# SSM tables: last sums of the X table on TensorE and ScalarE, wide Y products, attention masks and turns in halves

## The chip, the cores, the metric

One core of one Trainium2 chip. The time is that of one execution on the device in microseconds (us), smaller is better; every run here counted as fast but one, of the kernel before in the third and fourth group of experiments (530.97 us, over 1.5% above the fastest of its group); it is left out of the ratios. Times of runs and of the profile differ a little: the profiled run of the kernel before took 526.4 us (span 524.6), the median of its timed runs is 528.6.

## The reference

Two kinds of layer alternate, twice each, on x of 2048 positions and 512 channels (cut to what matters):

```python
def _A_ref(u, A_re, A_im, B_re, B_im, C_re, C_im, log_dt, Dskip):   # SSM convolution
    dt = jnp.exp(log_dt)[:, None]
    ...
    P = jnp.exp(logdA[:, :, None] * l[None, None, :])
    K = jnp.einsum("dn,dnl,dn->dl", Cc, P, dB).real                 # filter of 2048 taps, N = 128 modes
    ...
    y = irfft(rfft(u, 2 * L) * rfft(K, 2 * L))[:L]                   # long convolution
    return y + u * Dskip

def _B_ref(x, wqkv, wo):                                            # 32 heads, window 8, dilation 2
    ...

x = x + _A_ref(_layernorm(x), ...)
x = x + _B_ref(_layernorm(x), ...)
x = x + _A_ref(_layernorm(x), ...)
x = x + _B_ref(_layernorm(x), ...)
```

## The kernel before

The filter K is built in the first layer only. For each of eight groups of 64 channels (tables 0 to 7) VectorE builds a table X (32 powers), a base of a table Y (16 powers) and three times two products of that base; TensorE contracts X with Y in 256 small matmuls (the contraction), and ScalarE copies what comes of it to KTq (its evacuation). Beside it runs the convolution: transform matmuls (`s1`), Z copies on ScalarE, DMA transposes (`turn`), 16 matmuls of the second step (`s2`), copies to Kt (filter) or to xc and W (input), filter products pa and pb on VectorE (`products`), inverse matmuls, VT copies, final matmuls.

```python
def turn(nc, zt, Z, g0, n):
    for r in range(2):
        nc.sync.dma_start_transpose(zt[:, r, 0:n * 128]..., Z[:, r, g0:g0 + n, :]...)

# Conv: all of it draws on one PSUM pool, psA, of three buffers
def s1(self, rhs_j, n, drow=None):
    Z = self.z.tile([128, 2, 16, 128], BF, name="Z", tag="Z")          # two buffers before
    for jq in range(NJ // 4):
        ps = self.pst([128, 2, 16, 32])                                # psA
        ...                                                            # 8 matmuls
        self.evac("z", Z[:, :, 0:n // 8, jq * 32:(jq + 1) * 32], ps[:, :, 0:n // 8, :])   # ScalarE
    return Z

# Tables
def double(self, T, m, lev, hc):                                       # HALF = 8
    for e0 in range(0, m, HALF):
        ...
        nc.vector.tensor_tensor(v(ta), src, self.mult(self.MA, lev, hc, mm), ALU.mult)
        nc.vector.tensor_tensor(v(tb), src, self.mult(self.MB, lev, hc, mm), ALU.mult)
        nc.vector.tensor_tensor(T[...], ta[...], tb[:, ::-1, ...], ALU.add)

def half(hc, between=None):
    Xt, Y, Y2 = T.build(hc)                                            # Y: one buffer, X: two
    ...
    T.x_part(Xt, hc); T.y_base(Y, hc); T.y_products(Y, Y2, hc)
    r = between() if between is not None else None                     # the next s1, turn, s2
    with tc.high_priority():
        T.contract(Xt, Y, Y2, hc)                                      # frees Y
    return r

for dc in range(4):
    Kt = half(dc * 2, (lambda: k_fft(dc - 1)) if dc > 0 else None)
    if dc > 0:
        VT = cv.finish(dc - 1, xcs.pop(dc - 1), Kt, Xr, dc < 3)        # products, inverse, final
    if dc < 3:
        half(dc * 2 + 1, mid)                                          # mid: u_fft(dc + 1)
```

The order of instructions on an engine is chosen when the kernel is built, by a scheduler with priorities; at run time each engine works through its own list in that order.

## Time and profile before

| | before |
|---|---|
| median of three runs (lowest, highest) | 528.58 us (528.37, 529.04) |
| span of the profiled run, mean granted TensorE clock | 524.6 us, 0.934 |
| busy share: TensorE, VectorE, ScalarE | 73%, 82%, 67% |
| first Kt copy of table 7, here called the end of the table stage | 228.7 us |

```profile
PE 31%; DVE 28%; ACT 7%; DMA 5%; issue 5%; POOL 2%; SPq 2%; ACTq 0%; DVEq 0%; POOLq 0%
```

ScalarE is busy for only 2 to 6 tenths from slice 6 to slice 17, in the stage, and in many of these slices the clock falls to 6 to 8 tenths. The chain goes through TensorE and VectorE in nearly equal parts.

### The profile page before, as it was taken

To read this page: it belongs to the slowest core of one execution; us is meant where nothing else is said; L and a number is where in the kernel's file an instruction comes from. 1 tells how busy PE (TensorE), PEld (TensorE's weight loads), DVE (VectorE), ACT (ScalarE), POOL (GpSimd) and SP (SyncE) were. 2 spreads that over 40 slices of the span, in tenths; PEclk is the share of its full clock that TensorE was granted. 3 is DMA by queue.
4 is the path that set the end of the run, shared out by engine and by line. 5 is a ranking of instruction groups with operands and counts; after the bars stand their busy time and mean duration, and the time that the engine had idled before them with its cause. 6 is when DMAs were issued, how large, how long until landed. Compare 5 with 4: busy or idle time off the path is not lost.

```text
span 524.6 us, 15316 instructions
## 1 busy us (share of the span) xinstructions
PE 383.4 (73%) x6456; PEld 255.8 (49%) x6518; DVE 432.8 (82%) x974; ACT 350.1 (67%) x422; POOL 83.3 (16%) x135
## 2 busy tenths in 40 slices
PE   0200466568469555879898999987799989999996
PEld 0100324346246423656565565655566646666674
DVE  4999999989998998969696566887689999666663
ACT  3999825636265543635676777867788777888872
POOL 0000000000000003051146411134000214911110
PEclk9999998779688967979999899998899999999999
DMA  8301044363446257531437743424397004633532
GB/s 266 144 1 40 1 101 79 65 109 126 105 75 155 44 121 136 191 40 49 164 99 147 153 107 81 72 18 172 73 197 161 1 11 94 126 107 84 101 93 92
DMA packets 104826, 52.52 MB, mean 100 GB/s; under 512 B 86004, under 2 KB 100469, under 8 KB 103477
## 3 DMA queue, kind: packets, MB, share of 16 engines
q1 hardware_dynamic: 103044, 50.88, 42.2%
q8 instruction: 51, 0.84, 0.7%
q10 hardware_dynamic: 1584, 0.39, 0.4%
q0 software_dynamic: 128, 0.26, 0.1%
q14 instruction: 19, 0.15, 0.1%
HBM read 17.96 MB, written 8.13 MB: 50 GB/s over the span
## 4 chain that ended last, share of the span: by engine, by line
PE 31%; DVE 28%; ACT 7%; DMA 5%; issue 5%; POOL 2%; SPq 2%; ACTq 0%; DVEq 0%; POOLq 0%
PE psG L1090 5%; ACT PT L1127 5%; PE psG L1107 4%; PE S L1124 4%; PE O L1143 3%; DVE Ytab L660 3%; DVE Y2tab L662 3%; PE psG L1182 3%; DMA zt<-Z 3%; DVE ln_st_b L216 2%; DVE ta L623 2%; PE S L1182 2%; DVE tb L624 2%; DMA xt<-xq 2%; POOL XU L1262 1%
## 5 line engine op out<-in xcount | busy, mean ns | idle before, releaser
L1127 ACT ACTIVATE PT<-S 128x1824 bf16<-128x1824 f32 x72 | 121.7, 1690 | 35.1 <-PE S L1124 34.6
L1090 PE MATMUL psG<-XU,wqk 128*128 128x512 bf16 x196 | 56.3, 384 | 2.6 <-issue 1.5
L1095 DVE CAST st<-psG 128x512 bf16<-128x512 f32 x56 | 38.5, 688 | 21.0 <-PE psG L1090 20.5
L1143 PEld LDWEIGHTS <-PT 128*128 128x128 bf16 x1152 | 38.9, 96 | 13.0 <-DVE on L1151 1.5
L1107 PE MATMUL psG<-wv,XU 128*128 128x256 bf16 x288 | 40.7, 274 | 0.2 <-DVE st L1095 0.2
L1143 PE MATMUL O<-V,PT 128*128 128x17 bf16 x1120 | 38.9, 171 | 2.0 <-DVE on L1151 1.3
L311 PE MATMUL psA<-X,sb_F 128*128 128x128 bf16 x128 | 13.8, 242 | 36.4 <-ACT X L724 35.2
L311 PEld LDWEIGHTS <-sb_F 128*128 128x128 bf16 x256 | 16.9, 105 | 44.1 <-issue 41.8
L1124 PEld LDWEIGHTS <-KS 32*128 32x128 bf16 x1152 | 20.5, 93 | 28.4 <-issue 23.3
L298 ACT CAST Z<-psA 128x1024 bf16<-128x1024 f32 (+1 forms) x32 | 28.8, 987 | 7.5 <-PE psA L311 7.5
L679 PE MATMUL psk<-Ytab,Xtab 128*32 128x64 bf16 x1024 | 24.0, 209 | 12.0 <-issue 6.8
L1124 PE MATMUL S<-QS,KS 32*128 32x114 bf16 x1152 | 28.1, 211 | 6.1 <-DMA KS<-st 2.8
L336 PE MATMUL psA<-zt,sb_C 128*128 128x512 bf16 x30 | 14.9, 524 | 23.3 <-DMA zt<-Z 23.3
L1151 DVE TENSOR_TENSOR on<-O,rd 128x256 bf16<-128x256 f32 x70 | 29.7, 425 | 2.4
L682 PE MATMUL psk<-Y2tab,Xtab 128*32 128x48 bf16 x1024 | 23.3, 205 | 11.2 <-issue 9.1
L660 DVE TENSOR_TENSOR Ytab<-Ytab,MA 128x2048 bf16<-128x2048 bf16 (+1 forms) x33 | 30.6, 929 | 0.2
L662 DVE TENSOR_TENSOR Y2tab<-Ytab,MB 128x2048 bf16<-128x2048 bf16 (+1 forms) x33 | 30.6, 928 | 0.0
L688 ACT CAST KTq<-psk 128x1024 bf16<-128x1024 f32 (+1 forms) x9 | 8.3, 918 | 33.1 <-issue 32.5
L637 POOL MEMSET Xtab<- 128x64 bf16 x8 | 1.6, 200 | 180.2 <-PE psk L682 161.4
L1107 PEld LDWEIGHTS <-XU 128*128 128x128 bf16 x288 | 25.3, 98 | 6.9 <-issue 0.2
L682 PEld LDWEIGHTS <-Xtab 128*32 128x32 bf16 x1024 | 20.9, 102 | 15.7 <-issue 14.8
L679 PEld LDWEIGHTS <-Xtab 128*32 128x32 bf16 x1024 | 21.4, 107 | 13.0 <-issue 12.2
(252 smaller groups left out, 1060.8 us busy)
## 6 DMA issues: line engine op xcount, KB each, us to landing
kt_scratch<-Kt SPq DMA_DIRECT2D x4, 1024.0 KB, 3.9
Kt<-kt_scratch SPq DMA_DIRECT2D x4, 1024.0 KB, 5.0
QS<-st SPq DMA_DIRECT2D x58, 64.0 KB, 1.9
KS<-st SPq DMA_DIRECT2D x58, 64.0 KB, 1.9
X<-in_A_u_dram SPq DMA_DIRECT2D x4, 512.0 KB, 5.5
out_dram<-X SPq DMA_DIRECT2D x16, 128.0 KB, 1.7
k_scratch<-KTq SPq DMA_DIRECT2D x7, 256.0 KB, 2.5
KT<-k_scratch SPq DMA_DIRECT2D x7, 256.0 KB, 2.8
```

What stands on the lines that cost most here:

```text
L311: nc.tensor.matmul(o, F1[:, j, r, :], rhs_j(j), start=True, stop=not dk)
L660: nc.vector.tensor_tensor(v(Y[:, :, :, q * EYB:(q + 1) * EYB, :]), src, vm(self.mult(self.MA, lev, hc, EYB)), ALU.mult)
L662: nc.vector.tensor_tensor(v(Y2[:, :, :, (q - 1) * EYB:q * EYB, :]), src, vm(self.mult(self.MB, lev, hc, EYB)), ALU.mult)
L679: nc.tensor.matmul(psk[32 * g:32 * g + 32, ds, :], xs, Y[:, m // 2, h, :, t], start=(m == 0), stop=False, skip_group_check=True)
L682: nc.tensor.matmul(psk[32 * g:32 * g + 32, ds, EYB:], xs, Y2[:, 1 - m // 2, h, :, t], start=False, stop=(m == 3), skip_group_check=True)
L1090: nc.tensor.matmul(ps[:], wqk[:, ct, f0:f0 + 128], xnT[:, ct, par, UF + h * 512:UF + h * 512 + 512], start=(ct == 0), stop=(ct == 3))
L1095: eng(t[:], ps[:])
L1107: nc.tensor.matmul(ps[:].rearrange("p h d -> p (h d)"), xnT[:, ct, par, NQ * b + 1:NQ * b + 1 + NK], wv[:, ct, fp * 256:fp * 256 + 256], s ...
L1124: nc.tensor.matmul(S[:, i, sl * NQ:(sl + 1) * NQ], KS[r, e, f2, b * NQ + 1:b * NQ + 1 + NK], QS[r, e, f2, UF + b * NQ:UF + b * NQ + NQ], s ...
L1127: nc.scalar.activation(pt[:, 0:16 * NQ].rearrange("k (i x) -> k i x", i=4), S[:, :, 0:4 * NQ], ACT.Exp, scale=DH ** -0.5)
L1143: nc.tensor.matmul(O[:, x * 8 + i * 2 + e, :], pt[:, c0:c0 + 128], V[:, par * NB + b, (fp * 2 + f2) * 8 + i * 2 + e, :], start=True, stop= ...
L1151: nc.vector.tensor_tensor(on.rearrange("q (h d) -> q h d", d=DH), O[:, :, 0:DH], rd[:].unsqueeze(2).to_broadcast([128, 16, DH]), ALU.mult)
```

## The change

The intent is to take work off VectorE, which has the highest busy share. Its parts: (a) three operations of the coefficients move into a wait at the start; (b) another layout of Y and of the multipliers lets two products of 6144 elements replace six of 2048; (c) the last X doubling becomes two multiplies of 2048 into X and a buffer `xb` of its own, whose sum TensorE forms with an identity and ScalarE copies back (tables 1 to 7); (d) the second X column is copied by ScalarE; (e) in the attention layer the mask loads come two at a time and the transposes of late key rows are issued in halves at two steps. To make room, Z gets one buffer instead of two. The core of the diff:

```diff
+    def double_last(self, X, lev, hc, cv):
+        nc, m = self.nc, EX // 2
+        tb = cv.z.tile([128, 2, HD, m, 2], BF, name="xb", tag="xb")
+        ...
+        nc.vector.tensor_tensor(X[top half], src, self.mult(self.MA, lev, hc, m), ALU.mult)
+        nc.vector.tensor_tensor(tb, src, self.mult(self.MB, lev, hc, m), ALU.mult)
+        if hc == 0:
+            nc.vector.tensor_tensor(top, top, tb[:, ::-1]..., ALU.add)
+            return
+        for c in range(2):
+            ps = cv.pst([128, 2, 512])                       # psA, as all transforms
+            for q in range(2):
+                for k, t in ((0, X[top half]), (1, tb[:, 1 - c, hs])):
+                    nc.tensor.matmul(ps[:, q, :], cv.C["ident"][:], t..., start=(k == 0), stop=(k == 1))
+            nc.scalar.copy(X[:, c, :, m:, :]..., ps[:]...)
...
-        for lev in range(1, 5):
+        for lev in range(1, 4):
             self.double(X, 1 << lev, 6 + lev, hc)
+        self.double_last(X, 10, hc, cv)
...
-        cv = Conv(nc, tc, es, C, X, psA, ())
+        cv = Conv(nc, tc, es, C, X, psA, (), zbufs=1)
...
-                if 1 <= t <= 4 and Wt["todo"] or t == 8 and Wt["todo"]:
-                    Wt["todo"].pop()()
-                for g, steps in ((2, (1, 2, 4, 6)), (3, (4, 5, 6, 8))):
+                for _ in range({1: 2, 2: 2, 8: 1}.get(t, 0)):
+                    if Wt["todo"]:
+                        Wt["todo"].pop()()
+                for g, steps in ((2, (1, 2, (3, 5), 6)), (3, (4, 5, (6, 7), 8))):
```

More of the change, by code (lines that the diff above doesn't have):

```diff
@@ L518, in ladder @@
     nc.vector.tensor_tensor(ws[:], tb[:], rnd[:], ALU.subtract)
+    t1, t2 = tmp("t1"), tmp("t2")
+    nc.vector.tensor_tensor(t1[:], raw["C_re"][:], raw["B_re"][:], ALU.mult)
+    nc.vector.tensor_tensor(t2[:], raw["C_im"][:], raw["B_im"][:], ALU.mult)
+    nc.vector.tensor_tensor(t1[:], t1[:], t2[:], ALU.subtract)
     sh = tmp("sh")
@@ L540, in coefs @@
     def coefs():
-        t1 = tmp("t1")
-        t2 = tmp("t2")
-        nc.vector.tensor_tensor(t1[:], raw["C_re"][:], raw["B_re"][:], ALU.mult)
-        nc.vector.tensor_tensor(t2[:], raw["C_im"][:], raw["B_im"][:], ALU.mult)
-        nc.vector.tensor_tensor(t1[:], t1[:], t2[:], ALU.subtract)
         nc.vector.tensor_tensor(quad[:, :, 0, :], t1[:], dt_bc, ALU.mult)
@@ L565, in multipliers @@
             return
-        nc.scalar.copy(MA[:, i], src[:, 0].unsqueeze(2).to_broadcast([128, 8, 2, 64]))
+        nc.scalar.copy(MA[:, :, i], src[:, 0].unsqueeze(2).to_broadcast([128, 8, 2, 64]))
         conj = 7 <= i <= 10
-        nc.scalar.activation(MB[:, i, :, 0, :], src[:, 1], ACT.Copy, scale=-1.0 if conj else 1.0)
-        nc.scalar.activation(MB[:, i, :, 1, :], src[:, 1], ACT.Copy, scale=1.0 if conj else -1.0)
+        nc.scalar.activation(MB[:, :, i, 0, :], src[:, 1], ACT.Copy, scale=-1.0 if conj else 1.0)
+        nc.scalar.activation(MB[:, :, i, 1, :], src[:, 1], ACT.Copy, scale=1.0 if conj else -1.0)
     cur = LAM
@@ L608, in mult, with pair @@
     def mult(self, M, lev, hc, n):
-        return (M[:, lev, hc].rearrange("n c (h t) -> n (c h) t", t=2).unsqueeze(2)
+        return (M[:, hc, lev].rearrange("n c (h t) -> n (c h) t", t=2).unsqueeze(2)
                 .to_broadcast([128, 2 * HD, n, 2]))
+    def pair(self):
+        return self.wk.tile([128, 2, 2, HD, HALF * 2], BF, name="tab", tag="tab")
     def double(self, T, m, lev, hc):
@@ L616, in double @@
             mm = min(m, HALF)
-            ta = self.wk.tile([128, 2, HD, HALF * 2], BF, name="ta", tag="ta")
-            tb = self.wk.tile([128, 2, HD, HALF * 2], BF, name="tb", tag="tb")
+            both = self.pair()
+            ta, tb = both[:, 0], both[:, 1]
             def v(t):
-                return t[:].rearrange("n c h (e t) -> n (c h) e t", t=2)[:, :, 0:mm, :]
+                return t.rearrange("n c h (e t) -> n (c h) e t", t=2)[:, :, 0:mm, :]
             src = T[:, :, :, e0:e0 + mm, :].rearrange("n c h e t -> n (c h) e t")
@@ L626, in double, with x_part @@
                                     ta[:, :, :, 0:mm * 2], tb[:, ::-1, :, 0:mm * 2], ALU.add)
+    def double_last(self, X, lev, hc, cv):
+        nc, m = self.nc, EX // 2
+        tb = cv.z.tile([128, 2, HD, m, 2], BF, name="xb", tag="xb")
+        src = X[:, :, :, 0:m, :].rearrange("n c h e t -> n (c h) e t")
+        nc.vector.tensor_tensor(X[:, :, :, m:, :].rearrange("n c h e t -> n (c h) e t"), src,
+                                self.mult(self.MA, lev, hc, m), ALU.mult)
+        nc.vector.tensor_tensor(tb[:].rearrange("n c h e t -> n (c h) e t"), src, self.mult(self.MB, lev, hc, m), ALU.mult)
+        if hc == 0:
+            top = X[:, :, :, m:, :].rearrange("n c h e t -> n c h (e t)")
+            nc.vector.tensor_tensor(top, top, tb[:, ::-1].rearrange("n c h e t -> n c h (e t)"), ALU.add)
+            return
+        for c in range(2):
+            ps = cv.pst([128, 2, 512])
+            for q in range(2):
+                hs = slice(16 * q, 16 * q + 16)
+                for k, t in ((0, X[:, c, hs, m:, :]), (1, tb[:, 1 - c, hs])):
+                    nc.tensor.matmul(ps[:, q, :], cv.C["ident"][:], t.rearrange("n h e t -> n h (e t)"), start=(k == 0),
+                                     stop=(k == 1))
+            nc.scalar.copy(X[:, c, :, m:, :].rearrange("n h e t -> n h (e t)"),
+                           ps[:].rearrange("n q (h x) -> n (q h) x", x=2 * m))
     def build(self, hc):
-        nc = self.nc
-        Y = self.ty.tile([128, 2, HD, EY, 2], BF, name="Ytab", tag="Ytab")
-        Y2 = self.ty.tile([128, 2, HD, EY - EYB, 2], BF, name="Y2tab", tag="Y2tab")
+        Y = self.ty.tile([128, EY // EYB, 2, HD, EYB, 2], BF, name="Ytab", tag="Ytab")
+        Y2 = self.ty.tile([128, EY // EYB - 1, 2, HD, EYB, 2], BF, name="Y2tab", tag="Y2tab")
         X = self.tx.tile([128, 2, HD, EX, 2], BF, name="Xtab", tag="Xtab")
         return X, Y, Y2
-    def x_part(self, X, hc):
+    def x_part(self, X, hc, cv):
         nc = self.nc
@@ L638, in x_part @@
         nc.gpsimd.memset(X[:, 1, :, 0, :], 0.0)
-        nc.vector.tensor_copy(X[:, :, :, 1, :].rearrange("n c h t -> n (c h) t"),
-                              self.nu[:, hc].rearrange("n c (h t) -> n (c h) t", t=2))
-        for lev in range(1, 5):
+        (nc.vector.tensor_copy if hc == 0 else nc.scalar.copy)(
+            X[:, :, :, 1, :].rearrange("n c h t -> n (c h) t"),
+            self.nu[:, hc].rearrange("n c (h t) -> n (c h) t", t=2))
+        for lev in range(1, 4):
             self.double(X, 1 << lev, 6 + lev, hc)
+        self.double_last(X, 10, hc, cv)
@@ L644, in y_base @@
     def y_base(self, Y, hc):
-        self.nc.vector.tensor_copy(Y[:, :, :, 0, :].rearrange("n c h t -> n (c h) t"),
-                                   self.cb[:, hc].rearrange("n c (h t) -> n (c h) t", t=2))
+        nc = self.nc
+        nc.vector.tensor_copy(
+            Y[:, 0, :, :, 0, :].rearrange("n c h t -> n (c h) t"),
+            self.cb[:, hc].rearrange("n c (h t) -> n (c h) t", t=2))
         for lev in range(4):
-            self.double(Y, 1 << lev, lev, hc)
+            self.double(Y[:, 0], 1 << lev, lev, hc)
@@ L650, in y_products @@
     def y_products(self, Y, Y2, hc, h0=0, h1=HD):
-        nc = self.nc
-        if h1 - h0 == HD:
-            views = [(lambda t: t.rearrange("n c h e t -> n (c h) e t"), lambda m: m)]
-        else:
-            views = [(lambda t, c=c: t[:, c, h0:h1], lambda m, c=c: m[:, c * HD + h0:c * HD + h1]) for c in range(2)]
-        for q, lev in ((1, 4), (2, 5), (3, LV48)):
-            for v, vm in views:
-                src = v(Y[:, :, :, 0:EYB, :])
-                nc.vector.tensor_tensor(v(Y[:, :, :, q * EYB:(q + 1) * EYB, :]), src,
-                                        vm(self.mult(self.MA, lev, hc, EYB)), ALU.mult)
-                nc.vector.tensor_tensor(v(Y2[:, :, :, (q - 1) * EYB:q * EYB, :]), src,
-                                        vm(self.mult(self.MB, lev, hc, EYB)), ALU.mult)
+        nc, n = self.nc, EY // EYB - 1
@@ new lines, in y_products @@
+        whole = hc > 0 and h1 - h0 == HD
+        for lev in ((4,) if whole else (4, 5, 6)):
+            k = n if whole else 1
+            for dst, M in ((Y[:, lev - 3:lev - 3 + k], self.MA), (Y2[:, lev - 4:lev - 4 + k], self.MB)):
+                for cs in ((slice(0, 2),) if h1 - h0 == HD else (slice(0, 1), slice(1, 2))):
+                    shape = [128, k, (cs.stop - cs.start) * (h1 - h0), EYB, 2]
+                    nc.vector.tensor_tensor(
+                        dst[:, :, cs, h0:h1].rearrange("n q c h e t -> n q (c h) e t"),
+                        Y[:, 0:1, cs, h0:h1].rearrange("n q c h e t -> n q (c h) e t").to_broadcast(shape),
+                        M[:, hc, lev:lev + k, cs, 2 * h0:2 * h1].rearrange("n q c (h t) -> n q (c h) t", t=2)
+                        .unsqueeze(3).to_broadcast(shape), ALU.mult)
@@ L678, in contract @@
                     if m % 2 == 0:
-                        nc.tensor.matmul(psk[32 * g:32 * g + 32, ds, :], xs, Y[:, m // 2, h, :, t],
+                        nc.tensor.matmul(psk[32 * g:32 * g + 32, ds, :].rearrange("p (q e) -> p q e", e=EYB), xs, Y[:, :, m // 2, h, :, t],
                                          start=(m == 0), stop=False, skip_group_check=True)
                     else:
-                        nc.tensor.matmul(psk[32 * g:32 * g + 32, ds, EYB:], xs, Y2[:, 1 - m // 2, h, :, t],
+                        nc.tensor.matmul(psk[32 * g:32 * g + 32, ds, EYB:].rearrange("p (q e) -> p q e", e=EYB), xs, Y2[:, :, 1 - m // 2, h, :, t],
                                          start=False, stop=(m == 3), skip_group_check=True)
@@ L700, in kernel_and_first_conv @@
         mt = es.enter_context(tc.tile_pool(reuse_waits="tile", name="k_mt", bufs=1))
-        MA = mt.tile([128, 11, 8, 2, 64], BF, name="MA")
-        MB = mt.tile([128, 11, 8, 2, 64], BF, name="MB")
+        MA = mt.tile([128, 8, 11, 2, 64], BF, name="MA")
+        MB = mt.tile([128, 8, 11, 2, 64], BF, name="MB")
         cb = mt.tile([128, 8, 2, 64], BF, name="cb")
@@ L735, in half @@
                 T.y_base(Y, hc)
-                T.x_part(Xt, hc)
+                T.x_part(Xt, hc, cv)
             else:
-                T.x_part(Xt, hc)
+                T.x_part(Xt, hc, cv)
                 T.y_base(Y, hc)
@@ L783, in kernel_and_first_conv @@
         Xt, Y, Y2 = T.build(7)
-        T.x_part(Xt, 7)
+        T.x_part(Xt, 7, cv)
         side = T.tx.tile([128, 4096], BF, name="side", tag="Xtab")
@@ L1252, in late @@
                             ln_b.norm(xq[g][:, i], X[:, slot(m0 + i), :], m0 + i, nc.gpsimd)
-                    elif t == steps[2]:
-                        xt = xq[g, 1] = ld.tile([128, 16, 128], BF, name="xt", tag="xt")
-                        for h in range(2):
-                            nc.sync.dma_start_transpose(xt[:, 8 * h:8 * h + 8],
-                                                        xq[g][:, 2 * h:2 * h + 2].rearrange("p i d -> p (i d)"))
+                    elif t in steps[2]:
+                        h = steps[2].index(t)
+                        if h == 0:
+                            xq[g, 1] = ld.tile([128, 16, 128], BF, name="xt", tag="xt")
+                        nc.sync.dma_start_transpose(xq[g, 1][:, 8 * h:8 * h + 8],
+                                                    xq[g][:, 2 * h:2 * h + 2].rearrange("p i d -> p (i d)"))
                     elif t == steps[3]:
```

## The prediction

> **What bounds the kernel now.** I read the page first (busy share by slice, the chain that ended last), then the busy time by stretch, then the timelines of VectorE, TensorE and ScalarE for 36 to 225 us, where the change lies. The tables are built there: eight of them (0 to 7), each an X part, a Y base and Y products on VectorE, then 256 small matmuls ("the contraction") that release the single Y buffer.
>
> ```profile
> PE   0200466568469555879898999987799989999996
> DVE  4999999989998998969696566887689999666663
> 131.00:151.00 20.00, 11.27 (x310) 6.97 (x311) 19.42 (x36) 9.39 (x11) 0.24 (x2) 0.74 0.40 88
> ```
>
> The first two lines are busy tenths of the span in 40 slices: VectorE is at nine tenths up to about 220 us, TensorE is not. The third is one table (columns: stretch, length, then busy us of PE, PEld, DVE, ACT, POOL, clock, DMA): VectorE 19.42 of 20.00 us. One would say "bound by VectorE", but the second loop must be looked at too. VectorE first:
>
> ```profile
> 134.99 0.69 DVE L623 TENSOR_TENSOR ta<-Xtab,MA 128x1024 bf16<-128x1024 bf16 x1
> ...
> 138.26 0.23 DVE L645 COPY Ytab<-cb 128x128 bf16<-128x128 bf16 x1
> ...
> 139.18 0.27 DVE L623 TENSOR_TENSOR ta<-Ytab,MA 128x128 bf16<-128x128 bf16 x1
> ...
> 144.13 1.23 DVE L660 TENSOR_TENSOR Ytab<-Ytab,MA 128x2048 bf16<-128x2048 bf16 x1
> 145.28 1.22 DVE L662 TENSOR_TENSOR Y2tab<-Ytab,MB 128x2048 bf16<-128x2048 bf16 x1
> ...
> 150.95 0.29 DVE L623 TENSOR_TENSOR ta<-Xtab,MA 128x256 bf16<-128x256 bf16 x1
> ```
>
> The last X doubling runs from 134.99 to 139.18 (4.19 us, two copies included), the Y base to 144.13 (4.95), six products to 150.95 (6.82). A table without other work takes 20.14 us.
>
> Now the other loop. One contraction ends at 182.7; then:
>
> ```profile
> 182.83 1.01 ACT L688 CAST KTq<-psk 128x1024 bf16<-128x1024 f32 x1 [4.44 <-issue]
> 183.74 1.02 ACT L298 CAST Z<-psA 128x1024 bf16<-128x1024 f32 x1
> 188.05 1.03 PE L336 MATMUL psA<-zt,sb_C 128*128 128x512 bf16 x2 [5.17 <-DMA zt<-Z]
> 194.47 1.61 PE L311 MATMUL psA<-KT,sb_F 128*128 128x128 bf16 x23
> 196.88 0.21 PE L679 MATMUL psk<-Ytab,Xtab 128*32 128x64 bf16 x4 [0.27 <-DVE Ytab L660]
> ```
>
> ScalarE evacuates the contraction and the last Z; the transposes come back; 16 matmuls and 24 of the next transform follow; only then, in TensorE's order, the next contraction. It waited 0.27 us for VectorE, the same place gave 0.54 us at 149.95 and 0.66 us at 176.73. So the convolution's loop through TensorE, ScalarE and DMA is shorter than VectorE's by only 0.3 to 2 us a table. The two are balanced, and a gain on VectorE alone is capped there.
>
> **What the Trainium skill says.** "VectorE: DVE Perf Modes", section "The TRN2 errata", has a fixed cost for each VectorE instruction beside a per-element part. The trace agrees: start to start 0.60 us for 1024 elements, 1.14 for 2048, hence 0.53 per 1024 and 0.07 fixed. Its "perf-mode tier table" gives 1224 ns for a bf16 tensor_tensor of 2048; the trace has 1220, so the products are in the fast mode already and merging them can save only the fixed part. "TensorE: Matmul & The Clock Gate", section "The HAM clock gate", gives 427 ns a 512-column matmul cold and 216 warm: the trace has 0.43 and 0.22 in one group at 143.9 to 146.9. "PSUM — Partial Sum Buffer", section "Engine vs sequencer instructions", says that ScalarE and VectorE queues are strict FIFO and matmuls keep program order. The trace agrees: one transform matmul waiting for its transpose held back 252 contraction matmuls until 108.1 us. My argument rests on this.
>
> **The change part by part.**
>
> *Last X doubling.* Six operations of 1024 (4.19 us with copies) become two multiplies of 2048 (2 x 1.14), a Y copy and a dependency gap: about 2.5. Saves 1.7 us of VectorE in tables 1 to 7. Table 0 keeps the sum on VectorE as one wide add and saves 0.7.
>
> *Wide products.* Two of 6144: 0.07 + 6 x 0.533 = 3.27 each, 6.54 against 6.82. Saves 0.28 in tables 1 to 6.
>
> *Coefficients.* Three operations of 0.6 move into the wait for the input at 7 to 9 us: 1.8 us of VectorE. ScalarE is busy without a break from 13.3 to 61.3, and table 0's u transform hangs on it, so I expect little of this at the end. X's second column moves to ScalarE behind that block: table 1 then waits some 4 us for it.
>
> VectorE's sum: 7 x 1.7 + 6 x 0.28 + 0.7 + 1.8 = 16 us.
>
> *What it adds.* In each of seven tables eight 512-column matmuls (1.7 us warm) and two ScalarE copies of 1024 (0.95 each, as the Z copies), on psA, whose three buffers the transforms use in turn. In the built kernel's order the sums stand behind the previous stage's matmuls and ahead of the next transform. Start of sums to X ready: 3.0 us. They also move transforms: in tables 3 to 6 one Z copy precedes the contraction's evacuation and three follow it, where three or all four preceded it.
>
> *The loop after.* From one contraction's end: evacuation and three Z copies 3.9, transposes and 16 matmuls 9.2 (9.1 and 9.4 to 9.8 in the trace), sums 3.0, contraction 4.6: 20.7 us, against VectorE's new 18.2. Replaying with these terms: contraction 0 ends at 68.3 (before 70.1), 1 at 90.7 (91.1), 2 at 107.9 (113.2; the stall on the transpose named above goes, as the order no longer puts it there), 3 at 132 (136.0), 4 at 152.6 to 154 (154.7). So the early tables gain 4 to 5 us and it is lost by table 4.
>
> *The expensive place.* In table 5 VectorE's order now has the eight filter products pa/pb after the Y products; before, they stood in the Y base. The inverse transform needs them, and the sums and contraction 5 stand behind it on TensorE. Y products of table 5 end at about 165; pa/pb 6.4 more; from the last pa to the contraction's end 13.7 to 14.3 (168.4 to 182.7 in the trace): 184.5 to 187, against 182.7. VectorE has finished X6 by then and waits 7 to 9 us for the Y buffer. Contraction 6 follows 20.7 later, at 205 to 208 (202.6). Table 7's pa/pb also come after most products and its sums after the inverse: stage end 8 to 11 us later than before; I take 8.5, the low side, as several waits could overlap.
>
> *Masks and turns.* In the first attention layer TensorE waits for key rows that queue behind mask loads and two transposes issued together:
>
> ```profile
> 286.28 0.23 PE L1124 MATMUL S<-QS,KS 32*128 32x114 bf16 x4 [1.77 <-DMA KS<-st]
> 286.83 0.33 PE L1124 MATMUL S<-QS,KS 32*128 32x114 bf16 x12 [0.32 <-DMA KS<-st]
> 293.17 0.53 PE L1124 MATMUL S<-QS,KS 32*128 32x114 bf16 x16 [0.68 <-DMA KS<-st]
> ```
>
> That is 2.8 us; TensorE is busy 16.6 of 20 us here and 19.2 in the same part of the second layer, which has no mask loads. I expect 2.5 us back in the first layer, nothing in the second. The bytes are the same.
>
> Sum: 528.6 + 8.5 - 2.5 = 534.6.
>
> **The rivals.** *VectorE is the only bound.* Then most of 16 us comes through, with the masks about 512. For it: the busy row. Against: the 0.27 to 0.66 us waits, and the longer ScalarE chain. I give it one chance in ten. *Partial.* The early gain of 4 to 5 us stays and the later loop hides the sums better than I think, because ScalarE has 9 us free of 20 and a contraction can start on the first half of X: 525 or so. For it: whoever chose the split of Z copies, and the scheduler, saw room there. One in three. *Worse.* The wide product's extra stride loses the fast mode (then 6.4 us instead of 3.27, six tables, 38 us) or the contraction's four-run operand slows: 545 and more. Against: the innermost pairs stay adjacent. Under one in ten. *My chain:* about half.
>
> **Range and chances.** 0.5 x 534.6 + 0.33 x 525 + 0.1 x 512 + 0.07 x 550 = 530, and I say 531. Range 520 to 541: from a little better than "partial" to the pessimistic end of the chain (11 - 1). Two per cent is 518.0 or 539.2: faster 0.10, slower 0.15, same 0.75.
>
> **What would show it.** Right: wide products near 3.3 us; VectorE's busy time down by 10 to 14 us while its waits before the Y copy for the contraction grow from 3.3 us in all to 15 or more, the longest at table 6; contraction 2 ending 4 to 5 us earlier, contraction 5 and 6 later than before; the 1.77 us wait for key rows gone. Wrong: contraction 6 ending before 200 us (VectorE did bound), wide products at 6 us, or TensorE's wait for key rows unchanged. The prediction as a whole fails if the sums fit into ScalarE's free time without moving the Z copies.

## More of the kernel before

The prediction shows the rows of TensorE and VectorE in the busy view. Here are the rows of ScalarE and of the granted clock (tenths, 40 slices of 13.1 us), and then the chain of work that ended last, by engine:

```profile
ACT  3999825636265543635676777867788777888872
...
PEclk9999998779688967979999899998899999999999
```

## The result

| | before | after |
|---|---|---|
| median (lowest, highest) | 528.81 us (528.37, 529.67), 4 runs | 541.90 us (540.69, 543.41), 4 runs |
| profiled: span, mean granted clock | 524.6 us, 0.934 | 541.6 us, 0.924 |
| VectorE busy | 432.8 us | 418.2 us |
| end of the table stage | 228.7 us | 246.2 us |
| from there to the end | 295.9 us | 295.4 us |

Ratios in this document are the mean time of one kernel's runs over the mean of the other's runs of the same rounds, so not quite the ratio of the medians quoted. The change is slower: 1.0247 (95% interval 1.0218 to 1.0276). VectorE did 14.6 us less, and the kernel took 13 us more. In the profiled pair all of it is lost in the table stage. (This pair, 526.4 and 543.4 us, lies 17 us apart, the medians 13; so what is read from the two profiles may be up to 4 us too much.)

The same rows of the changed kernel's page, and the chain that ended last:

```profile
PE   0200665877557746779989989998789989989997
...
DVE  5999689979969487725788666788689999766674
ACT  3999744755453546364577768876788877878872
...
PEclk9999997879676968597999999998899999999999
```

```profile
PE 43%; DVE 20%; ACT 17%; DMA 11%; issue 6%; SPq 3%; POOL 0%; ACTq 0%; DVEq 0%
```

VectorE, at nine tenths before in nearly every slice up to 220 us, now has slices of 6, of 4 and one of 2 in the stage. In the chain VectorE's share went from 28 to 20%, and ScalarE went from 7 to 17, DMA from 5 to 11: the loop through TensorE, ScalarE and DMA now sets the pace. One turn of it, from the timelines, first ScalarE (start, duration, operation), then the DMA queue of SyncE, then TensorE:

```profile
190.71 1.01 ACT L715 CAST KTq<-psk 128x1024 bf16<-128x1024 f32 x1 [3.76 <-PE psk L709]
191.62 2.85 ACT L298 CAST Z<-psA 128x1024 bf16<-128x1024 f32 x3
```

```profile
194.49 5.94 SPq L270 DMA_TRANSPOSE zt<-Z  x4
```

```profile
190.55 1.50 PE L311 MATMUL psA<-X,sb_F 128*128 128x128 bf16 x17
198.21 1.04 PE L336 MATMUL psA<-zt,sb_C 128*128 128x512 bf16 x2 [6.16 <-DMA zt<-Z]
...
200.70 0.63 PE L337 MATMUL psA<-zt,sb_C 128*128 128x512 bf16 x1
...
203.22 0.38 PE L337 MATMUL psA<-zt,sb_C 128*128 128x512 bf16 x1
```

Contraction 5 ends at 190.6. Only then do three of the four Z copies run (191.62): in ScalarE's list they stand behind the contraction's evacuation (KTq), and TensorE too has about half of this transform's 32 matmuls behind the contraction (190.55). A transform that is begun ahead of a contraction and ended behind it is called split below. (The first of the three copies waited for its place on ScalarE, as its matmuls were done at 186.2; the other two had to wait for their matmuls. No run tests the two orders apart.) The transposes start at 194.49, the second step waits 6.16 us for them, and its first matmuls run at the low clock (200.70 takes 0.63, 203.22 takes 0.38). Then come the sums, which belong to table 6. In the kernel before, three or all four Z copies stood ahead of the evacuation.

VectorE in the same turn and before it:

```profile
158.35 0.22 DVE L671 COPY Ytab<-cb 128x128 bf16<-128x128 bf16 x1 [3.97 <-PE psk L709]
...
166.84 3.35 DVE L686 TENSOR_TENSOR Y2tab<-Ytab,MB 128x6144 bf16<-128x6144 bf16 x1
170.11 0.68 DVE L383 TENSOR_TENSOR pa<-xc,Kt 128x1024 bf16<-128x1024 bf16 x1
...
176.36 0.69 DVE L383 TENSOR_TENSOR pa<-xc,Kt 128x1024 bf16<-128x1024 bf16 x1
...
179.47 1.23 DVE L635 TENSOR_TENSOR Xtab<-Xtab,MA 128x2048 bf16<-128x2048 bf16 x1
184.85 1.23 DVE L637 TENSOR_TENSOR xb<-Xtab,MB 128x2048 bf16<-128x2048 bf16 x1 [4.16 <-PE psA L647]
190.65 0.22 DVE L671 COPY Ytab<-cb 128x128 bf16<-128x128 bf16 x1 [4.57 <-PE psk L709]
```

Waits of 3.97, 4.16 and 4.57 us: for the Y buffer, for `xb` (which the sums of table 5 still read, behind the inverse) and for the Y buffer again. From 170.11 on stand the filter products pa and pb, after the wide products of table 5 (166.84). The wide products take 3.35 us, those of 2048 take 1.23.

The key rows in the first attention layer (TensorE, as in the prediction's last lines):

```profile
296.72 0.23 PE L1151 MATMUL S<-QS,KS 32*128 32x114 bf16 x4 [0.43 <-DMA KS<-st]
...
314.54 0.40 PE L1151 MATMUL S<-QS,KS 32*128 32x114 bf16 x8 [1.46 <-DMA KS<-st]
```

The wait of 1.77 us is gone, but one of 1.46 us stands further on; over the kernel TensorE waits 3.1 us for key rows after and 2.8 before.

### The profile page after: what moved, and what is told of

It reads as the page before. It is cut to its first block, busy times and chain, and to the rows that moved or that the text cites. A ratio compares the mean times of both kernels' runs of the same rounds, so it can differ in the third digit from the quotient of the medians.

```text
span 541.6 us, 15407 instructions
## 1 busy us (share of the span) xinstructions
PE 398.5 (74%) x6509; PEld 261.8 (48%) x6574; DVE 418.2 (77%) x912; ACT 364.5 (67%) x443; POOL 82.4 (15%) x135
## 4 chain that ended last, share of the span: by engine, by line
PE 43%; DVE 20%; ACT 17%; DMA 11%; issue 6%; SPq 3%; POOL 0%; ACTq 0%; DVEq 0%
PE psG L1117 6%; DMA zt<-Z 6%; PE S L1151 4%; ACT PT L1154 3%; PE O L1170 3%; PE psG L1134 3%; SPq L270 3%; DVE ln_st_b L216 3%; DMA KS<-st 3%; PE psG L1209 3%; PE S L1209 2%; PE psk L706 2%; PE psA L337 2%; ACT Z L298 2%; PE psA L339 2%
## 5 line engine op out<-in xcount | busy, mean ns | idle before, releaser
L311 PEld LDWEIGHTS <-sb_F 128*128 128x128 bf16 x256 | 18.2, 110 | 43.9 <-issue 41.3
L336 PE MATMUL psA<-zt,sb_C 128*128 128x512 bf16 x30 | 15.7, 566 | 31.5 <-DMA zt<-Z 31.4
L1151 PEld LDWEIGHTS <-KS 32*128 32x128 bf16 x1152 | 20.7, 93 | 28.5 <-issue 20.2
L298 ACT CAST Kt<-psA 128x1024 bf16<-128x1024 f32 x14 | 14.0, 1013 | 26.2 <-PE psA L339 26.2
L686 DVE TENSOR_TENSOR Ytab<-Ytab,MA 128x512 bf16<-128x512 bf16 (+2 forms) x21 | 28.3, 1372 | 0.2
L686 DVE TENSOR_TENSOR Y2tab<-Ytab,MB 128x512 bf16<-128x512 bf16 (+2 forms) x21 | 28.3, 1370 | 0.0
L709 PEld LDWEIGHTS <-Xtab 128*32 128x32 bf16 x1024 | 19.7, 98 | 16.6 <-issue 15.9
L1191 POOL COPY oT<-oS 128x684 bf16<-128x684 bf16 x20 | 15.1, 756 | 72.2 <-DMA oS<-on 72.2
L216 DVE BATCH_NORM_STATS2 ln_st_b<-X 128x6 f32<-128x128 bf16 (+2 forms) x80 | 24.0, 357 | 2.2 <-ACT X L432 2.2
```

Source lines behind the costliest of these rows:

```text
L216: self.nc.vector.bn_stats(self.st[:, j, part, :], X[:, slot(j), a:b])
L298: self.nc.scalar.copy(dst, src)
L311: nc.tensor.matmul(o, F1[:, j, r, :], rhs_j(j), start=True, stop=not dk)
L686: nc.vector.tensor_tensor(dst[:, :, cs, h0:h1].rearrange("n q c h e t -> n q (c h) e t"), Y[:, 0:1, cs, h0:h1].rearrange("n q c h e t -> n ...
L709: nc.tensor.matmul(psk[32 * g:32 * g + 32, ds, EYB:].rearrange("p (q e) -> p q e", e=EYB), xs, Y2[:, :, 1 - m // 2, h, :, t], start=False, ...
L1151: nc.tensor.matmul(S[:, i, sl * NQ:(sl + 1) * NQ], KS[r, e, f2, b * NQ + 1:b * NQ + 1 + NK], QS[r, e, f2, UF + b * NQ:UF + b * NQ + NQ], s ...
```

## The experiments

The stage end in the tables is the start of the first Kt copy of table 7 in the profile. Runs of one group shared a chip and the runs of the kernel before; the third and fourth group were on the same chip and share all but one of these.

**Theories.** *Order:* the sums and what they displace lengthen the loop through TensorE, ScalarE and DMA, by the place where they stand. *Work:* the sums cost TensorE and ScalarE too much wherever they stand. *Rival A:* the single Z buffer delays the transforms. *Rival B:* the new Y layout slows the contraction. *Attention:* the masks and turns cost.

| run | median us | ratio to before (95%) | stage end us |
|---|---|---|---|
| before (profile) | 528.6 | 1 | 228.7 |
| after | 541.90 | 1.0247 (1.0218 to 1.0276) | 246.2 |
| e1 sum on VectorE | 532.17 | 1.0057 (1.0009 to 1.0106) | 235.5 |
| e2 attention only | 527.80 | 0.9981 (0.9939 to 1.0023) | 228.5 |
| e3 no last X change | 528.31 | 0.9990 (0.9927 to 1.0053) | 230.1 |
| e4 sums after the transform | 520.95 | 0.9841 (0.9804 to 0.9878) | 225.2 |
| e5 sums first, unsplit | 526.16 | 1.0008 (0.9937 to 1.0078) | 226.8 |
| e6 sum on VectorE, e4's order | 520.53 | 0.9896 (0.9834 to 0.9958) | 219.6 |
| e7 before, e4's order | 521.21 | 0.9917 (0.9846 to 0.9989) | 220.8 |
| e8 e4 with table 7 too | 520.62 | 0.9908 (0.9841 to 0.9976) | 225.6 |
| e9 masks only | 527.50 | 0.9986 (0.9960 to 1.0012) | 227.9 |
| e10 turns only | 531.43 | 1.0053 (1.0015 to 1.0091) | 229.6 |
| e11 e6, masks, old turns | 518.26 | 0.9805 (0.9774 to 0.9837) | 220.3 |
| e12 e6, old attention | 519.00 | 0.9823 (0.9792 to 0.9854) | 223.4 |
| e13 e5, late products in table 5 | 532.35 | 1.0057 (1.0017 to 1.0097) | 236.8 |
| e14 e5, split in tables 3 to 6 | 538.25 | 1.0173 (1.0134 to 1.0213) | 241.1 |

The groups are e1 to e4, e5 to e8, e9 to e12, and e13 with e14. The kernel before itself spread from 522.4 to 529.1 in the second group (median 526.3), so its ratios are the least certain.

**e1, the sum on VectorE.**

```diff
-        if hc == 0:
+        if True:
             top = X[:, :, :, m:, :]...
```

> The changed kernel, but the last X sum of every table is the wide VectorE add that table 0 has (no sums on TensorE, no X copies on ScalarE; the single Z buffer, the wide Y products, the coefficients and the attention halves stay). My theory (the sums lengthen the loop through TensorE, ScalarE and DMA): VectorE gets 7 x 1.14 us back, the loop loses 7 x 3 us, so 518 to 528 us and the VectorE waits for Kt and for the Y buffer fall below 15 us in sum. Rival A (the single Z buffer delays the transforms) and rival B (the wide products with their new Y layout slow the contraction): stays at 536 or more.

Measured 532.2: 10 us better than the changed kernel, but outside what my theory allowed, and no rival said it either. The build gave it an order of its own: contraction 5 came in the middle of an inverse, and table 7's first half came in pieces. It waited 17.6 us for Kt and 4.2 us for the Y buffer, so my 15 us failed too. It showed that taking an instruction out also changes the order of the others.

**e2, the attention part alone** (the last part of the diff above, on the kernel before).

> The kernel before with only the attention part of the change (mask loads two at a time at steps 1 and 2, key turns in halves). The prediction's term says 2.5 us less, 526. The trace of the changed kernel (wait for key rows 3.1 us where it was 2.8) says nothing, 528 to 529. If the attention part is what costs, 532 or more.

Measured 527.8, 0.9981: no effect is seen. The interval reaches from 3.2 us in favour to 1.2 against, so the 2.5 us of the prediction are neither seen nor excluded; that this part makes the loss of 13 us is.

**e3, all but the last X doubling** (the doubling and the copy of the second X column as before).

```diff
-        for lev in range(1, 4):
+        for lev in range(1, 5):
             self.double(X, 1 << lev, 6 + lev, hc)
-        self.double_last(X, 10, hc, cv)
```

> The changed kernel, but with the X doubling and the copy of the second column as before (six operations of 1024 on VectorE, no xb). Single Z buffer, wide products, coefficients and attention halves stay. My theory: no sums on TensorE, so about the kernel before less 0 to 4 us: 523 to 529. Rival A (single Z buffer) or rival B (Y layout): 536 or more.

Measured 528.3, as my theory said. The single Z buffer and the new Y layout are in this kernel, so rivals A and B can't explain 13 us. It also shows that coefficients and wide products, some 3.5 us of VectorE by the prediction's count, gave nothing visible in this order.

**e4, the same instructions, the sums behind the next transform.**

```diff
+        self.sums = lambda: self.last_sums(X, tb, m, cv)     # instead of emitting them at once
...
             self.evac("z", Z[...], ps[...])
+        if self.hook is not None:                            # at the end of s1
+            self.hook()
+            self.hook = None
...
+            if hc > 0:
+                cv.hook = T.sums
             r = between() if between is not None else None
```

> The changed kernel with the same instructions, but the sums of a table stand on TensorE behind the next transform's matmuls instead of ahead of them, so all four Z copies come first on ScalarE, then the two X copies, then the contraction and its evacuation. If the order is what costs (Z copies held back behind the evacuation, s2 waiting 6 us for its transposes): 528 to 536, and the waits of L336 for the transposes fall from 31 to below 22 us. If it is the work of the sums itself, wherever it stands: 540 to 545.

Measured 521.0, lower than I expected, and faster than both kernels: 21 us from order alone. The contraction needs the X copies, these need the sums, and the sums now need a psA buffer that a Z copy frees; so the build can no longer put the contraction into the middle of a transform. The same turn as above, ScalarE, SyncE's queue and TensorE:

```profile
172.52 3.78 ACT L298 CAST Z<-psA 128x1024 bf16<-128x1024 f32 x4
176.14 2.00 ACT L657 CAST Xtab<-psA 128x1024 bf16<-128x1024 f32 x2
183.72 1.01 ACT L723 CAST KTq<-psk 128x1024 bf16<-128x1024 f32 x1 [5.59 <-issue]
```

```profile
176.33 5.92 SPq L270 DMA_TRANSPOSE zt<-Z  x4
```

```profile
183.51 0.39 PE L339 MATMUL psA<-zt,sb_C 128*128 128x512 bf16 x1
...
186.75 0.38 PE L342 MATMUL psA<-zt,sb_C 128*128 128x512 bf16 x1
```

All four Z copies are done at 176.3 and the transposes start at 176.33, 7 us ahead of the evacuation at 183.72. They run while TensorE contracts, and the second step at 183.51 waits for nothing and runs warm throughout. The waits of the second step for its transposes, whole kernel (us in all, times, longest), in the order before, after, e4:

```profile
PE psA L336 <- DMA zt<-Z: 23.3, 7, 5.2
```

```profile
PE psA L336 <- DMA zt<-Z: 31.4, 7, 6.2
```

```profile
PE psA L339 <- DMA zt<-Z: 7.5, 2, 4.2
```

31.4 us became 7.5 (the line numbers shift by three), and the mean granted clock of the profiled runs rose from 0.924 to 0.974. The theory *work* falls. The clock is not the gain: e6, e7 and e8 below are as fast, with 0.929, 0.941 and 0.948.

**e5, the sums first as in the change, but no transform split.** e4 moved two things at once, so this one moves one back. TensorE's order is fixed by hand within each table:

```diff
-            r = between() if between is not None else None
-            with tc.high_priority():
-                T.contract(Xt, Y, Y2, hc)
-            return r
+            cv.hook = lambda: T.contract(Xt, Y, Y2, hc)      # called at the end of s1 (table 0: as before)
+            with tc.manual_schedule(engines={mybir.EngineType.PE}):
+                return between()
```

> The changed kernel with the sums where the change has them (ahead of the next transform's matmuls), but the contraction of tables 1 to 6 fixed behind all of that transform's matmuls, so all four Z copies stand ahead of the contraction's evacuation. Same instructions. Run e4 took 21 us off by moving the sums; it changed two things at once. If the split Z copies are the larger part (transposes start after the contraction instead of under it, L336 waits 31 us): 525 to 531, L336 waits below 15 us. If the sums' 3 us ahead of each transform are the larger part: 534 to 540.

Measured 526.2, within what I gave for the split being the larger part. The wait:

```profile
PE psA L339 <- DMA zt<-Z: 15.4, 8, 4.2
```

It is half the 31.4 us, though not below the 15 that I gave, and with the next line's waits it is 26.7 of 38.6 (8.3 in e4). In the same group the sums behind the transform (e8, 520.6) are 5.5 us faster, so that is the price of the sums ahead of each transform, with what the build moved on VectorE besides.

**e6, the sum on VectorE in e4's order** (the edits of e1 and e5 together).

> As e1 (last sum on VectorE in all tables), but TensorE's order fixed as in e4: transform, contraction, second step, inverse. e1 came out at 532 where I expected 518 to 528; if its own order (contraction between the second step and the inverse, table 7 in pieces) is why, this is 519 to 525. Against e4 (521) it tells what the sums on TensorE are worth in the right order: if VectorE bounds, e4 is faster by up to 7 us; if not, they are equal or this is faster.

Measured 520.5, within the range. e1's 532 was its order. Against e8 of the same group (520.6) the sums on TensorE are worth nothing in total in the right order. The stage ended 6 us earlier here (219.6 against 225.6), but the profiled runs took 292.6 to 297.8 us from there to the end, and the total does not show the 6 us. Why not stays open. (e12, with the same tables, ended the stage at 223.4, so this mark varies too.)

**e7, the kernel before in e4's order** (e5's edit on the kernel before).

> The kernel before with nothing of the change but TensorE's order fixed as in e4 (no transform matmul or Z copy left behind the contraction). It tells whether e4 owes its gain to the order alone. VectorE has 19.4 of 20 us here, so the order should give little: 525 to 529. If the order alone is the gain: 519 to 523.

Measured 521.2, where I expected 525 to 529: a miss. With every VectorE instruction of the kernel before (431.9 us busy), the stage ends 8 us earlier and VectorE has no wait above 0.3 us from 69 to 220 us. e6, e7 and e8 lie within 0.7 us. So the kernel before was losing to its order as well.

**e8, e4 with table 7's sums behind its transform too.**

```diff
         T.x_part(Xt, 7, cv)
-        T.sums()
...
+        cv.hook = T.sums
         Kt, zts = k_fft(3, 0, 1)
```

> e4 with table 7's sums too behind its transform. In e4 table 7's X copies stood ahead of four Z copies (2 us). Expected 1 to 3 us below e4: 517 to 520. If VectorE's products bound table 7, no change: 520 to 522.

Measured 520.6, e4 within the spread: no change.

**e9 to e12, the attention parts apart, and candidates.** e9 is the kernel before with the `Wt["todo"]` lines of the diff alone, e10 with the turns alone. e11 is e6 with the old turns, e12 is e6 with old turns and old mask loads.

> The kernel before with only the mask loads moved (two at steps 1 and 2, one at 8). In the profiles the first attention layer (first to last exponential) took 86.6 and 87.6 us without the attention part and 83.3 to 86.8 (mean 85.0, eight profiles) with it; the second took 81.8 without and 82.5 to 85.4 with it. If the masks give the first layer's 2 us and the turns cost the second layer's 1.5: first layer near 85, second 81.8, total 526 to 527 where before is at 528. If the masks give nothing: equal to before within 0.5 us.

> The kernel before with only the key turns in halves (steps 3 and 5, 6 and 7). If the halves cost the second layer (its second half is issued a step later, and TensorE waited 0.25 and 0.62 us for the copies into XU there): second layer 82.5 to 83.5, total 0 to 2 us above before. If the halves are free: second layer 81.8.

> A candidate: e6 (last sum one wide VectorE add, TensorE's order fixed) with the masks of the change but the turns as before. If the turns in halves cost the second layer 1.5 us, 518 to 520 where e6 was at 520.5; otherwise 520 to 522.

> e6 with the attention layers as before. If masks and turns cancel, equal to e6, 520 to 522; if the masks alone help, 1 to 2 us above e11. As only the tables differ from before here, the stage should end near 219.6 us as in e6 (before 228.7), and the total be 7 to 9 us below before if nothing after the stage gives it back.

Measured 527.5, 531.4, 518.3 and 519.0. The masks alone are equal to before within 0.4%; the turns alone cost some 2.8 us (1.0053; 0.8 to 4.8 by the interval), where I gave 0 to 2. My reading of the profiles failed: the first attention layer took 86.4 us with the masks (85 expected) and the second 83.3 (81.8 expected), so these durations vary by 1 to 2 us from profile to profile. Nor do the parts add up, as e2 with both was at 0.9981. At this size the attention part is not settled: no run shows the 2.5 us, and e2 alone does not exclude them; what is settled is that it did not make the loss. e11 and e12 differ by 0.7 us, which their spread covers. e11 was the fastest version tried: 518.3, 0.9805 of before.

**e13 and e14, the two halves of e5's gain.** Going from the change to e5 unsplit the Z copies, and with that the build also put table 5's filter products back into its Y base (and table 7's largely ahead of its products). e13 puts only the first of these product moves back, by fixing VectorE's order in table 5 (on TensorE the sums of table 5 stand behind the final matmuls, as in e5). e14 puts the split back, two copies of four behind the evacuation:

```diff
+                with tc.manual_schedule(engines={mybir.EngineType.DVE}):   # e13, table 5 only
+                    T.x_part(Xt, hc, cv); T.y_base(Y, hc); T.y_products(Y, Y2, hc)
+                    pre()                                                  # finish(1): pa, pb
...
+            cv.at = 1 if 3 <= hc <= 6 else 3                               # e14: contract after s1's second group
```

> e5 with one thing of the changed kernel put back: the eight filter products pa/pb of table 5 stand after its Y products on VectorE (the Z copies stay unsplit). The prediction's term for this place was 2 to 4 us later at contraction 5. If it holds, contraction 5 ends at 185 to 187 (182.8 in e5) and the total is 528 to 531 where e5 had 526. If the late products cost nothing without the split: 526 within a microsecond, and contraction 5 ends at 183.

> e5 with the other thing put back: in tables 3 to 6 the contraction stands between the halves of the next transform, so two Z copies come after its evacuation (in the changed kernel three of four). The build then also puts table 5's products after its Y products and table 7's between them, as in the changed kernel. If split and what follows from it are the whole difference of 16 us, 538 to 543; with e13's share taken off, the split alone is the rest. If neither matters, 526.

e13 measured 532.4, 1.3 us over the range I gave, with contraction 5 done 4 us later than I gave (2.5 us of its lateness against e5 stood already at contraction 4, 155.6 and 153.1, ahead of the edit). VectorE of e5, then of e13:

```profile
167.00 0.69 DVE L386 TENSOR_TENSOR pa<-xc,Kt 128x1024 bf16<-128x1024 bf16 x1
...
182.82 0.22 DVE L674 COPY Ytab<-cb 128x128 bf16<-128x128 bf16 x1 [1.44 <-PE psk L712]
```

```profile
167.75 0.68 DVE L386 TENSOR_TENSOR pa<-xc,Kt 128x1024 bf16<-128x1024 bf16 x1
...
175.15 0.68 DVE L387 TENSOR_TENSOR pb<-xc,Kt 128x1024 bf16<-128x1024 bf16 x1
...
183.54 1.22 DVE L640 TENSOR_TENSOR xb<-Xtab,MB 128x2048 bf16<-128x2048 bf16 x1 [5.85 <-PE psA L655]
191.07 0.22 DVE L679 COPY Ytab<-cb 128x128 bf16<-128x128 bf16 x1 [6.30 <-PE psk L717]
```

In e5 the last pa ends at 167.7, ahead of the wide products, and contraction 5 is done at 182.8. In e13 the products start at 167.75 and last until 175.8, the inverse, the final matmuls and the sums of table 5 wait for them, `xb` comes free only after 5.85 us, and the Y buffer at 191.07. From 161.2 to 167.75 VectorE had worked on the wide products, though the Kt copies for the filter products came from 160.70 on: it worked on the wrong thing first.

e14 measured 538.3, as expected for "split and what follows from it". The wait for the transposes is back:

```profile
PE psA L339 <- DMA zt<-Z: 28.7, 8, 5.3
```

In the built order of e14 table 5's filter products are late too, and table 7's stand among its Y products, so e14 less e13 is not the split alone. Nor is e13's cost a part of the change's that can be taken off as it is. From the evacuation of contraction 4 to that of 5, the stretch with the late products, e5 took 29.8 us, e13 35.6, but e14 32.1 and the changed kernel 32.3. In e13 the first Kt copy starts at 160.70 and the products at 167.75; in the changed kernel, where the split holds the transposes back, at 168.80 and 170.11. There the late products mostly wait for what the split makes late anyway.

## Why the prediction was wrong

It said 531 with a range to 541, and the median is 541.9; "slower by over 2%", given 0.15, came about.

**Right.** *The two loops are balanced and a gain on VectorE is capped:* VectorE's busy time fell by 14.6 us (10 to 14 said among the signs, 16 in the sum), the wide products take 3.28 us start to start (3.27 said), VectorE's waits before the Y copy grew to 13.5 us with the longest, 4.57, at table 6 (15 or more said, which they miss; longest at table 6), and the end came later. At table 6 it waited 4.16 us for `xb` and 4.57 for the Y buffer, 8.7 in all, where 7 to 9 was said for the Y buffer. *The places:* contractions 0, 1 and 2 ended at 68.9, 90.3 and 108.9 (68.3, 90.7, 107.9 said), so the early gain was there; contraction 5 came late. One reading was loose: in its "busy without a break from 13.3 to 61.3" ScalarE has a wait of 0.42 us at 18.53, without weight here.

**The terms that were too small, and one that was not.** All in the stage, where 8.5 us was said (an end at 237.2) and 17.5 came (246.2, in the profiled pair):
- *Between contractions 2 and 3*, 27.1 us against my 24.1: VectorE waited 2.78 us for Kt ahead of the first products, as the second step waited for its transposes, and contraction 3 ended at 136.0 where I had 132. From here on every time was some 4 to 6 us late. It is no matter of the split: the same stretch took 29.0 us in e5 and 27.6 in e4, and 24.2 and 23.9 in e6 and e7, which have no sums on TensorE (start to start of the evacuations). So it is 3 to 5 us longer where the sums stand on TensorE; how my 24.1 was made up the prediction does not show, and which of its parts was short stays open. By table 4 the gain was not only lost but reversed, 158.3 against 154.7 before.
- *Not the late products at table 5.* I saw them in the built order and gave them 2 to 4 us. Contraction 5 came 8 us later than before (190.6 against 182.7), but it set out from a contraction 4 at 158.3, where I had 152.6 to 154. From there to contraction 5 the kernel took 32.3 us, and my times leave 30.5 to 34.4; from the last pa to the contraction's end it took 13.6 (13.7 to 14.3 said). This term was right.
- *Table 7.* From contraction 6 to the stage end took 25.9 us before and 34.3 after, 8.4 us more; my 8.5 for the whole, after 2 to 5 us at contraction 6, left it 3 to 6. I took "the low side, as several waits could overlap". They followed one another. 5.2 of the 8.4 us lie ahead of the first Kt copy, which came 4.7 us after the evacuation of contraction 6 before (202.87 to 207.54) and 9.9 us after it now (211.91 to 221.78). The transposes of table 6's split transform are why; SyncE's queue before, then after:

```profile
199.12 6.30 SPq L270 DMA_TRANSPOSE zt<-Z  x4
```

```profile
215.69 5.41 SPq L270 DMA_TRANSPOSE zt<-Z  x4
```

Before, they started 3.6 us ahead of contraction 6's end (202.7), after, 3.9 us behind it (211.8).

**The step that failed.** The mechanism held, and nearly so did the turn of 20.7 us into which I had put the moved Z copies: the kernel took 22.2 us from contraction 3 to 4 and 21.2 from 5 to 6. What failed is the stage's sum, in two terms: the stretch from contraction 2 to 3 (24.1 us said, 27.1 measured), and that from contraction 6 to the stage end (3 to 6 us more than before said, 8.4 measured). For the second the prediction names table 7's products and sums and not the split of table 6's transform, though it had noted that tables 3 to 6 are split. What a split does was in the very lines that I showed, where the second step waits 5.17 us for its transposes: whatever stands behind the evacuation can't be transposed while TensorE contracts.

Nor did I ask what the turn would take without the split, and that is where most of the 21 us between the change and e4 lie: change 541.9; half the copies split (e14) 538.3; none split (e5) 526.2; the sums behind the transform as well (e4, e8) 521.0 and 520.6. From e5 to the change it is 16 us as medians and 13 as ratios to the kernel before in each group; this holds the split and what the build moved with it. e13 (no split, table 5's products late) was at 532.4, 6 us above e5 as medians, but 3 to 4 when each is set against the kernel before in its group; it shows what late products cost where Kt is ready, and is no step between e5 and e14. These runs lie in different groups, and a boundary may be off by 2 or 3 us; e5 against e8 is of one group, as is e13 against e14.

**The attention term.** 2.5 us less was said. The part gives 0.9981 alone, the wait for key rows as a whole did not fall (2.8 to 3.1 us), and from the stage end on the profiled pair differs by 0.5 us (295.9 and 295.4).

**The blend.** My own sum was 534.6. I moved it to 531, 3.6 us further off, by a third of weight on "partial", for the reason that ScalarE has 9 us free of 20 and that the scheduler saw room. Free time in the mean says nothing about the moment at which a copy is due. The prediction's last sentence named this condition, "if the sums fit into ScalarE's free time without moving the Z copies". They do fit, as e4 shows; but in the kernel as built the Z copies had moved, and the order of instructions, which I had, said so.

## What to carry to other kernels

Where two in-order engines share a loop, first ask what each long transfer has to hide under, and see that the instruction that starts it stands ahead of that in its queue. Only then count busy time: here fixing the order of unchanged work gave about as much (e7) as fixing it together with less VectorE work (e6). When a change adds instructions to an engine that a scheduler orders, compare the built order before and after and price each displacement as a term of its own.

## What the Trainium skill lacked or had wrong

- "Perfetto Trace Analysis", section "Identifying the Most-Contended Engine", says to optimise the engine of highest occupancy first. Here that was VectorE (82% busy); 14.6 us less of it came with 13 us more time, and with VectorE's work unchanged a new order of TensorE gave 0.9917 (e7). The page's section "Optimization Strategy" then looks for the gaps on that same engine; here the waits that mattered stood on TensorE (28.8 us for the transposes before, 14.0 in e7).
- "DMA: Bandwidth & Descriptors", section "Latency and other measured facts", gives 261 GB/s for a DMA transpose with a non-contiguous middle dimension. Four transposes of 128 x 1024 two-byte elements (1.05 MB) took 5.94 us in the changed kernel's queue and 5.92 in e4's, but the queue's rows end before the data land: the last one was issued at 199.2 and landed up to 3.7 us later, so all four took up to 8.4 us from 194.49 on, some 125 GB/s as an estimate from these. Whether the page's case has the same layout it does not say.
- No page says that the place of a PSUM copy in ScalarE's queue, and of its matmuls in TensorE's, can decide when DMA transposes start. The runs show it: transposes 3.9 us after the contraction's end (190.6 to 194.49) in the changed kernel and 7.2 us ahead of it (176.33 to 183.5) in e4, with 31.4 and 7.5 us of waiting.
